# An FFT filter and two MLPs: the inverse transform in program order, with GpSimd issuing only DMAs there

## The chip, the cores and the metric

The kernel runs on 1 core of one Trainium2 chip. The metric is the device time of one execution in microseconds; lower is better. The kernel before took 1181.16 us (median of 3 runs, 1179.31 to 1184.85).

## The reference

```python
X = np.fft.rfft(x, axis=1)                        # x: 2 x 3008 x 256
Yr = Xr @ w_r - Xi @ w_i + b_r
Yi = Xr @ w_i + Xi @ w_r + b_i
Y = softthreshold(Yr, 0.01) + 1j * softthreshold(Yi, 0.01)
y = np.fft.irfft(Y, n=3008, axis=1)               # 6016 tokens x 256
h = y @ w_in;  y = (h * sigmoid(1.702 * h)) @ w_out    # 256 -> 2048 -> 256
h = y @ w_in2; y = (h * sigmoid(h)) @ w_out2           # 256 -> 2048 -> 256
```

All of it is float32, and the weights and the filter come as inputs.

## The kernel before

Everything is one program on one core, in four stages. The **forward** stage and the **mid** stage (the 512-wide complex product, threshold, folds) come first; then comes the **inverse** stage, which this case is about, and then the **MLP** stage, which is most of the time.

The inverse runs 16 steps, counted here 0 to 15: two column halves q, two batches b, four products t. `inv_mm` (line 598 on) makes one step's product into two PSUM banks. Steps with t = 0 and 1 use one pool of four banks, those with t = 2 and 3 the other, so a step can only begin where the step four earlier (same t, one batch before) has had its banks read. A step of q = 0 is 16 float32 matmul records of 188 to 192 columns, one of q = 1 is 12 of 376. Its result is taken off by `inv_post`, one step later in the program: for t = 0 and 1 of q = 0 by a ScalarE copy to `eo` (line 639; there is one `eo` buffer) and two VectorE combinations into `rt` (lines 647 and 384); for t = 0 and 1 of q = 1 by two ScalarE copies to `rt` (line 634); for t = 2 and 3 by four VectorE operations on `ac` and `rt` (lines 658, 659). There is one `rt` buffer. When four steps of a batch are done, `inv_out` writes `yt`, the tokens of that batch half: two of its four parts as sums or differences (line 689, on VectorE or GpSimd by the table `ivf`), two as a ScalarE copy (line 691) onto which a GpSimd-issued accumulating DMA adds the other operand (line 693).

In the same stretch two other jobs go on. One converts MLP weights, unit by unit: a 512 KB load into `raw` on the SP queue (line 166; one buffer), a ScalarE operation (line 175), five VectorE operations (lines 180 to 184), an accumulating DMA (line 237), and then the split into a rounded `hi` and a remainder `lo`. For units of `wo` the remainder is a ScalarE negation and an accumulating DMA (lines 105 to 107); for units of `wi` it is a GpSimd subtraction (lines 109, 110) ahead of which stand four small VectorE sums (lines 212 to 215, into `tmp`). The other prepares the first token block of the MLP: `xsums` and `xprep` (lines 706 on) make seven inputs k = 0 to 6, each split in `hi` and `lo`; k = 2, 3 and 5 share the buffer `tmp`, which is updated between them (line 727). `xprep` with k = 0 to 3 is called in the steps that the table `xi` names (11, 12, 13, 15), with `lo` made by ScalarE and an accumulating DMA (lines 722, 723); k = 4, 6 and 5 are called inside the first MLP group, with `lo` made by a VectorE subtraction (line 725).

What sets the order: the mid stage is in program order on all engines. In the inverse only TensorE is; the instructions of the other engines are placed by a scheduler, which reaches across the borders of the steps and of the stages. So is the first group of the MLP. From the second group on all is in program order.

The inverse-stage matrices `m` of q = 1 (four loads of 564 KB on the SP queue, line 137) are called for in steps 1 and 3.

Of the kernel before, what the change touches and what calls it, by code (L numbers as in the profile page):

```python
# [8 lines left out]

F32 = mybir.dt.float32  # L10
CFG = {'lv0': 'V', 'lv': 'VVVVVPVVVVVP', 'dd0': 'VPVVPPPPPVVP', 'dd': 'VVVVVVVVVVPV', 'ths': 'VVVVPV', 'thf': 'VVVP', 'ivf': 'VVVPVVVV', 'cva': 'P', 'pol': 'PPPP', 'pil': 'P', 'mvl': 'PVVP', 'xl': 'V', 'xse': 'V', 'gl': 'VPPPPPPP', 'tf': [6, 9, 12], 'tm': [2, 6, 10], 'ti': [1, 4, 7, 10], 'kb': [0, 1, 1, 1, 1, 1, 1, 0], 'kr': [0, 1, 0, 1, 0, 1, 1, 0], 'fa': 3, 'xp': [2, 4, 4, 5], 'xq': [1, 4, 1], 'xs': 4, 'xi': [11, 12, 13, 15], 'xsi': 9, 'ca': 4, 'tl': True, 'fwd': 'Pool,SP', 'rest0': 'all', 'rest1': 'all', 'last1': 'all', 'inv': 'PE', 'mid': 'all', 'last0': 'all', 'thm': 'A', 'gl0': 'PVPVVVPV', 'gl2': 'PPPPPPPP', 'gl3': 'PPPPPPPV', 'xl0': 'V', 'xl1': 'V', 'pre': 14, 'pre2': 0, 'yd': 6, 'lvb': 6, 'mlp': 'none', 'pr': 'VVVP', 'pf': 'PV', 'eo': '0010', 'n32': 2, 'li': [8, 10], 'xa': 4, 'nhb': 6, 'ddb': 6, 'mlp1': 'all', 'mlp2': 'all'}
NUM = dict(li=[5, 6, 7, 8], n32=2, pk=4, ydp=2, lii=[1, 3], xd=4, nhb=6, tf=[5, 9, 13], tm=[1, 3, 5, 7, 9, 11], ti=[0, 2, 4, 6, 8, 10, 12, 14, 14, 15, 15], kb=[2] * 8, kr=1, fa=3, fe=2, pm=0, nf=4, lvb=6, ddb=8, ivb=1, eob=1, fsb=6, f1=3, f2=0, fm=[7, 8, 9], fi=[1, 1, 2, 2], pre=13, pre2=1, yd=3, psh=0, ie=[12], xp=[1, 3, 4, 5], xq=[1, 2, 2], xs=5, nw=4, xi=[14, 14, 15, 15], xsi=13, rw=2, ca=4, cc=2, tb=1, tmn=1)

DEF = dict(pr="V", pf="V", lv0="V", lv="VPP", dd0="VVVVVP", dd="VPV", mpl="PV", ths="VP", thf="VVPP", fsl="VP", ivf="PPVV", cva="P", pol="P", pil="P", mvl="V", xl="PPVVPPP", xl0="PPVVPPP", xl1="PPVVPPP", xse="VP", gl="P", gl0="P", gl2="P", gl3="P", wcl="V", thc="V", thm="V")
F32R = mybir.dt.float32r
# [1 line left out]
AF = mybir.ActivationFunctionType  # L17
# [4 lines left out]
P = 128  # L22
# [34 lines left out]
def spectral_mlp_kernel(ctx, tc, xin, mfwd, minv, wc, bias, w_in1, w_out1, w_in2, w_out2, outT):  # L57
    nc = tc.nc
# [187 lines left out]
    def window(k, done, now=False):  # L246
        for u, a in done:
            if u[0] == "in":
                sums, puts = place_in(u[1], u[2], a, E('pil', u[2]), sums_tmp)
                if now:  # L250
                    for f in (puts[0], *sums, puts[1]):
                        f()
                else:
                    fill.extend(sums + puts)
            else:
                place_out(u[1], u[2], a, "D")
        for _ in range(min(k, len(loaded))):
# [453 lines left out]
    def xprep(l, i, k, part=3):  # L711

        n = blocks[i][1]
        (b11, t3), (b21, b22) = xhalves(i)
        src = (b11, b21, xtmp[0], xtmp[0], t3, xtmp[0], b22)[k]
        if part & 1:
            xb[l, i, k] = tuple(slot(0, F32R, "x")[:, :n] for _ in range(2))
            nc.scalar.copy(xb[l, i, k][0], src)  # L718
        if part & 2:
            hi, lo = xb[l, i, k]  # L720
            if (l, i) == (0, 0) and k < N('xd'):
                nc.scalar.mul(lo, src, -1.0)
                nc.gpsimd.dma_start(out=lo, in_=src, accum_op=ALU.add)
            else:
                E('xl1' if l else 'xl0' if i == 0 else 'xl', k).tensor_sub(lo, src, r32(hi))  # L725
            if k in (2, 3):
                nc.vector.tensor_sub(xtmp[0], b22 if k == 2 else b21, xtmp[0])

    prev = None
    for q in range(2):  # L730
        for b in range(B):
            for t in range(4):
                ps = inv_mm(q, b, t)
                if prev is not None:
                    inv_post(*prev)
                    if ydone:
                        inv_out()
                prev = (q, b, t, ps)
                if 8 * q + 4 * b + t == N('pre'):
                    tc.keep_in_program_order(nc.scalar.preload_act_table(AF.Gelu_apprx_sigmoid))  # L740
                step = 8 * q + 4 * b + t
                if step in N('lii'):
                    load_m()
                if step == N('xsi'):
                    xsums(0, 0)
                for k in range(4):
                    if N('xi')[k] == step:
                        xprep(0, 0, k)
                if step in N('ti'):
                    tick(N('ti').count(step))  # L750
    inv_post(*prev)
    inv_out()

    region('mlp')


    acc = {}
# [134 lines left out]
    for at, (l, i, p) in enumerate(seq):  # L892
        if (l, i, p) in ((0, 0, 1), (0, 0, 2)):
            region(f'mlp{p}')
        if (i, p) == (1, 0):
            region(f'rest{l}')
        if (i, p) == (last, 0):
            region(f'last{l}')
        nxt = (l, i + 1) if i < last else (1, 0)
        more = p == NPR - 1 and (l, i) != (1, last)  # L900
        k = rate(at)

        def hook(h):
            if more:
                if h in (1, 2):
                    for x in ((0,), (1, 2))[h - 1]:
                        xprep(*nxt, x)
                if h == 3:
                    xprep(*nxt, 3, 1)
                if h == 4:  # L910
                    xprep(*nxt, 3, 2)
            if p == 0:
                for x in {1: (4,), 3: (6, 5)}.get(h, ()):
                    xprep(l, i, x)
            if h == 1 and p == NPR - 2 and (l, i) != (1, last):
# [166 lines left out]
```

## Time and profile before

| | |
|---|---|
| median of 3 runs | 1181.16 us (1179.31 to 1184.85) |
| the profiled execution | 1180.89 us, of which the span of the trace is 1179.0 us |
| busy: TensorE / ScalarE / VectorE / GpSimd | 98% / 66% / 54% / 43% of the span |
| forward and mid stage | 0 to 138.5 us |
| inverse stage on TensorE | 138.5 to 195.4 us |
| MLP stage | 195.4 us to the end |

The span is cut by the work of TensorE (PE in the rows; PEld is its weight load). In the MLP stage it waits for almost nothing; its idle time stands in the forward stage and in the two places where the inverse hands over to itself (at 165 us) and to the MLP (198 to 204 us). VectorE is DVE in the rows, ScalarE is ACT, GpSimd is POOL.

### The profile page before, as it was taken

To read this page: it belongs to the slowest core of one execution; us is meant where nothing else is said; L and a number is where in the kernel's file an instruction comes from. 1 tells how busy PE (TensorE), PEld (TensorE's weight loads), DVE (VectorE), ACT (ScalarE), POOL (GpSimd) and SP (SyncE) were. 2 spreads that over 40 slices of the span, in tenths; PEclk is the share of its full clock that TensorE was granted. 3 is DMA by queue.
4 is the path that set the end of the run, shared out by engine and by line. 5 is a ranking of instruction groups with operands and counts; after the bars stand their busy time and mean duration, and the time that the engine had idled before them with its cause. 6 is when DMAs were issued, how large, how long until landed. Compare 5 with 4: busy or idle time off the path is not lost.

```text
span 1179.0 us, 14496 instructions
## 1 busy us (share of the span) xinstructions
PE 1153.6 (98%) x5036; PEld 941.2 (80%) x5036; DVE 633.2 (54%) x968; ACT 773.2 (66%) x1455; POOL 507.8 (43%) x433
## 2 busy tenths in 40 slices
PE   7999988999999999999999999999999999999998
PEld 3758865887888878878889978888888888888897
DVE  6838897776556366465564552442532622523522
ACT  2467445777667667667677776676665766766755
POOL 2336364444444444434446755433333433433333
PEclk9999999999999999999999999999999999999999
DMA  7556468332221221121120100010000000000000
GB/s 268 180 99 144 148 117 159 75 86 45 57 57 32 70 63 46 36 72 36 41 76 24 58 10 27 1 37 1 1 37 1 16 21 1 36 1 1 36 1 32
DMA packets 37259, 66.30 MB, mean 56 GB/s; under 512 B 3393, under 2 KB 14657, under 8 KB 37186
## 3 DMA queue, kind: packets, MB, share of 16 engines
q1 hardware_dynamic: 25730, 46.28, 11.7%
q0 software_dynamic: 11456, 19.10, 9.6%
q8 instruction: 39, 0.64, 0.2%
q14 instruction: 34, 0.28, 0.1%
HBM read 35.92 MB, written 10.35 MB: 39 GB/s over the span
## 4 chain that ended last, share of the span: by engine, by line
PE 85%; DVE 5%; DMA 4%; ACT 3%; issue 2%; POOL 1%; SPq 0%; DVEq 0%; POOLq 0%; ACTq 0%
PE o L772 39%; PE x L800 35%; PE psm L515 5%; PE psf L354 4%; ACT yt L803 1%; PE psm L512 1%; DMA raw<-in_x 1%; DMA raw<-in_wo 1%; PE psi L354 1%; ACT g L805 1%; DMA raw<-in_wi 1%; DMA x<-tmp 1%; DVE lv L302 1%; DVE cv_c L180 0%; DVE g L810 0%
## 5 line engine op out<-in xcount | busy, mean ns | idle before, releaser
L810 POOL TENSOR_TENSOR g<-yt,g 128x512 fp32r<-128x512 f32 (+1 forms) x282 | 363.5, 1301 | 503.9 <-PE x L800 315.1
L772 PE MATMUL o<-g,wo 128*128 128x512 f32 (+1 forms) x2304 | 560.9, 385 | 0.6 <-DMA wo<-cv_a 0.6
L800 PE MATMUL x<-x,wi 128*128 128x512 f32 (+1 forms) x2016 | 500.9, 387 | 8.3 <-ACT yt L836 3.7
L772 PEld LDWEIGHTS o<-g,wo 128*128 128x128 f32 x2304 | 432.7, 188 | 82.4 <-DMA wo<-cv_a 1.0
L800 PEld LDWEIGHTS x<-x,wi 128*128 128x128 f32 x2016 | 377.4, 188 | 86.9 <-ACT yt L836 7.8
L803 ACT ACTIVATE yt<-yt 128x512 f32<-128x512 f32 (+1 forms) x288 | 179.0, 622 | 251.0 <-DVE yt L842 198.8
L805 ACT CAST g<-yt 128x512 fp32r<-128x512 f32 (+1 forms) x384 | 234.9, 612 | 12.1
L842 DVE TENSOR_TENSOR yt<-yt,x 128x512 f32<-128x512 f32 (+1 forms) x96 | 64.7, 674 | 215.2 <-PE x L800 214.5
L821 DVE TENSOR_TENSOR yt<-yt,x 128x512 f32<-128x512 f32 (+1 forms) x96 | 64.8, 675 | 165.6 <-ACT yt L819 160.0
L810 DVE TENSOR_TENSOR g<-yt,g 128x512 fp32r<-128x512 f32 (+1 forms) x102 | 71.4, 700 | 71.3 <-ACT g L805 70.5
L354 PE MATMUL psf<-m,xf 128*128 128x376 f32 (+2 forms) x208 | 58.9, 444 | 8.4 <-DVE xf L313 8.2
L845 DVE TENSOR_TENSOR yt<-yt,x 128x512 f32<-128x512 f32 (+1 forms) x96 | 64.8, 675 | 3.3 <-PE x L800 2.7
L725 DVE TENSOR_TENSOR x<-yt,x 128x512 fp32r<-128x512 f32 (+1 forms) x46 | 47.9, 1044 | 29.1 <-ACT x L718 29.1
L354 PEld LDWEIGHTS psf<-m,xf 128*128 128x128 f32 x208 | 38.1, 194 | 28.5 <-DVE xf L313 9.4
L803 ACT ACTIVATE yt<-x 128x512 f32<-128x512 f32 (+1 forms) x96 | 56.0, 583 | 0.2 <-PE x L800 0.2
L354 PE MATMUL psi<-m,f 128*128 128x376 f32 (+3 forms) x208 | 52.1, 406 | 3.9 <-DVE rt L384 3.9
L836 ACT COPY yt<-x 128x512 f32<-128x512 f32 (+1 forms) x96 | 55.8, 581 | 0.0
L819 ACT COPY yt<-x 128x512 f32<-128x512 f32 (+1 forms) x96 | 54.8, 570 | 0.9 <-POOL g L810 0.9
L834 ACT COPY yt<-x 128x512 f32<-128x512 f32 (+1 forms) x96 | 54.8, 571 | 0.0
L354 PEld LDWEIGHTS psi<-m,f 128*128 128x128 f32 x208 | 37.2, 194 | 17.4 <-DVE rt L384 4.8
L237 POOL DMA_DIRECT2D cv_a<-cv_c x32 | 30.4, 952 | 33.4 <-DVE cv_c L184 14.9
L394 ACT COPY xt<-psf 128x128 f32<-128x128 f32 (+2 forms) x96 | 18.2, 286 | 33.2 <-PE psf L354 33.0
(105 smaller groups left out, 838.9 us busy)
## 6 DMA issues: line engine op xcount, KB each, us to landing
raw<-in_wi SPq DMA_DIRECT2D x32, 256.0 KB, 3.2
cv_a<-cv_c POOLq DMA_DIRECT2D x32, 256.0 KB, 3.4
raw<-in_wo SPq DMA_DIRECT2D x16, 512.0 KB, 3.8
raw<-in_x SPq DMA_DIRECT2D x12, 512.0 KB, 5.0
xl<-xt POOLq DMA_DIRECT2D x20, 256.0 KB, 4.3
out_t<-yt SPq DMA_DIRECT2D x20, 256.0 KB, 2.0
m<-in_mf SPq DMA_DIRECT2D x4, 564.0 KB, 5.6
m<-in_mi SPq DMA_DIRECT2D x4, 564.0 KB, 8.6
```

The source lines that it names most:

```text
L354: nc.tensor.matmul(ps, hi[:, c : c + P], m[:, k, :w], start=i == 0, stop=i == last)
L515: nc.tensor.matmul(t, st, mv, start=n == 0 and k == 0, stop=n == 3 and grp == 1 and k == 2)
L772: nc.tensor.matmul(acc[h, mm], st, mv, start=first and k == 0, stop=last and k == 2)
L800: nc.tensor.matmul(ps, st, mv, start=first and m == 0, stop=m == 2, skip_group_check=True)
L803: nc.scalar.activation(g, g if src is None else src, func)
L805: nc.scalar.copy(gh, g)
L810: eng.tensor_sub(gl, g, r32(gh))
L819: nc.scalar.copy(y1, X)
L821: nc.vector.tensor_add(y1, y1, Y)
L836: nc.scalar.copy(y3, X)
L842: nc.vector.tensor_add(y2, y2, X)
L845: nc.vector.tensor_add(y3, y3, Z)
```

## The change

1. The inverse stage is in program order on every engine (`inv` from 'PE' to 'all'). The first MLP group stays with the scheduler.
2. GpSimd gets no arithmetic there. The split of `wi` units uses the way of the `wo` units ("D": two ScalarE operations and an accumulating DMA), and all sums of `inv_out` are VectorE's (`ivf` = 'V').
3. All seven `xprep` of the first block are called inside the inverse, in steps 9, 10, 8, 11, 12, 14, 13 for k = 0 to 6 (`xsums` in step 8), all with a DMA for `lo`; the update of `tmp` stands ahead of k = 3 and 5.
4. The weight units are spread otherwise: up to six queued VectorE operations are issued in each step (`pi`), and a load of `raw` is called for two steps behind the conversion, not with it.

```diff
-CFG = {... 'ivf': 'VVVPVVVV', ... 'xi': [11, 12, 13, 15], 'xsi': 9, ... 'inv': 'PE', ...}
+CFG = {... 'ivf': 'V', ... 'xi': [9, 10, 8, 11, 12, 14, 13], 'xsi': 8, ... 'inv': 'all', ...}
...
-                sums, puts = place_in(u[1], u[2], a, E('pil', u[2]), sums_tmp)
+                sums, puts = place_in(u[1], u[2], a, "D" if modes[0] else E('pil', u[2]), sums_tmp)
...
+        if (l, i) == (0, 0) and k in (3, 5):
+            nc.vector.tensor_sub(xtmp[0], b22 if k == 3 else b21, xtmp[0])
...
-            if (l, i) == (0, 0) and k < N('xd'):
+            if (l, i) == (0, 0):
                 nc.scalar.mul(lo, src, -1.0)
                 nc.gpsimd.dma_start(out=lo, in_=src, accum_op=ALU.add)
+                return
...
-                for k in range(4):
-                    if N('xi')[k] == step:
+                for k, at in enumerate(N('xi')):
+                    if at == step:
                         xprep(0, 0, k)
+                pump(N('pi'))
                 if step in N('ti'):
-                    tick(N('ti').count(step))
+                    ready = settle()
+                    window(0, ready)
+                    window(1, ())
+                if step - 2 in N('ti'):
+                    cv_load(1 - len(loaded))
...
-            if p == 0:
+            if p == 0 and (l, i) != (0, 0):
                 for x in {1: (4,), 3: (6, 5)}.get(h, ()):
                     xprep(l, i, x)
```

Three places show how the instructions move. Names are those of the program: `psi` is a product in PSUM, `raw_...` a weight unit, and lines behind the change are one to ten higher than before (648 was 647, 692 was 691, 721 was 718).

VectorE where the mid stage ends and the inverse begins, before:

```order
L647 TENSOR_TENSOR rt<-psi,eo 128x2x2x95
L548 TENSOR_TENSOR f_1288<-th 128x512
L180 TENSOR_SCALAR cv_c<-cv_c 128x512
L384 TENSOR_TENSOR rt<-psi,eo 128x4x94
L181 TENSOR_SCALAR cv_c<-cv_c 128x512
L658 TENSOR_TENSOR ac<-rt,psi 128x377 x2
```

and after:

```order
L548 TENSOR_TENSOR f_1288<-th 128x512
L180 TENSOR_SCALAR cv_c<-cv_c 128x512
L181 TENSOR_SCALAR cv_c<-cv_c 128x512
L182 SCALAR_TENSOR_TENSOR cv_a<-raw_1170,cv_c 128x512
L183 TENSOR_SCALAR cv_c<-cv_a 128x512
L184 SCALAR_TENSOR_TENSOR cv_c<-raw_1170,cv_c 128x512
L648 TENSOR_TENSOR rt<-psi,eo 128x2x2x95
L384 TENSOR_TENSOR rt<-psi,eo 128x4x94
```

The two combinations that free the first step's bank stood around the last fold and the first conversion; now all five conversions of `raw_1170` stand ahead of them.

ScalarE in the first steps of the inverse, before:

```order
L639 COPY eo<-psi 128x2x192 x3
L691 ACTIVATE yt<-ac 128x2x377
L691 COPY yt<-ac 128x2x376
L109 CAST wi_1349<-tmp 128x512
L175 ACTIVATE cv_c<-raw_1301 128x512
```

and after:

```order
L640 COPY eo<-psi 128x2x192
L175 ACTIVATE cv_c<-raw_1301 128x512
L640 COPY eo<-psi 128x2x192
L105 ACTIVATE wi_1346<-cv_a 128x384
L107 CAST wi_1346<-cv_a 128x384
L105 ACTIVATE wi_1346<-tmp 128x512
```

The operation that waits for the load of `raw_1301` now stands between the `eo` copies of steps 0 and 1. On the SP queue that load, which stood behind the four loads of `m`, now stands ahead of them.

GpSimd in the second half of the inverse after the change; between the subtractions for `wi_1219` and those of the MLP there are now 29 DMA issues in a row, where before there were 22 among six subtractions and sums:

```order
L106 DMA wo<-cv_a 128x512
L694 DMA yt<-ac 128x2x377
L694 DMA yt<-ac 128x2x188 x2
L726 DMA x<-tmp 128x512
L726 DMA x<-yt 128x512 x2
L237 DMA cv_a<-cv_c 128x512
L106 DMA wo<-cv_a 128x512
```

Here the three accumulates of a batch half, those of k = 2, 0 and 1 and two of the weights follow one another with nothing between.

## Rows read from the trace of the kernel before

**Rows 1.** The page, busy time, share and instructions by engine.

```profile
PE 1153.6 (98%) x5036; PEld 941.2 (80%) x5036; DVE 633.2 (54%) x968; ACT 773.2 (66%) x1455; POOL 507.8 (43%) x433
```

**Rows 2.** Busy time by stretch: stretch, length, each engine, clock, DMA share, GB/s.

```profile
core 0: us, PE busy (x) PEld busy (x) DVE busy (x) ACT busy (x) POOL busy (x), PEclk, DMA share, GB/s
153.00:166.00 13.00, 9.17 (x48) 7.93 (x49) 11.60 (x17) 4.25 (x8) 9.30 (x8) 1.00 0.64 120
166.00:170.00 4.00, 4.00 (x9) 2.15 (x8) 3.96 (x11) 2.16 (x5) 2.61 (x3) 0.57 0.74 184
...
196.00:204.00 8.00, 3.96 (x17) 2.64 (x16) 7.17 (x14) 4.08 (x7) 1.71 (x2) 1.00 0.59 134
204.00:208.00 4.00, 4.00 (x12) 3.11 (x11) 0.94 (x2) 2.96 (x6) 1.27 (x1) 0.57 0.00 0
```

**Rows 3.** Timeline of TensorE, start, length, shape, count, idle time before and releaser.

```profile
138.50 6.01 PE L354 MATMUL psi<-m,f 128*128 128x192 f32 x36
...
153.31 2.21 PE L354 MATMUL psi<-m,f 128*128 128x192 f32 x12 [0.43 <-DVE rt L384]
...
165.42 30.39 PE L354 MATMUL psi<-m,f 128*128 128x376 f32 x90 [3.52 <-DVE rt L384]
195.36 3.19 PE L800 MATMUL x<-x,wi 128*128 128x512 f32 x12
199.21 0.97 PE L800 MATMUL x<-x,wi 128*128 128x512 f32 x3 [0.66 <-ACT yt L819]
203.56 2.50 PE L800 MATMUL x<-x,wi 128*128 128x512 f32 x6 [3.39 <-DVE yt L821]
...
226.84 1.52 PE L800 MATMUL x<-x,wi 128*128 128x512 f32 x6
```

**Rows 4.** Timeline of VectorE, first steps of the inverse.

```profile
146.54 1.22 DVE L180 TENSOR_SCALAR cv_c<-cv_c 128x512 f32<-128x512 f32 x1
147.68 0.54 DVE L384 TENSOR_TENSOR rt<-psi,eo 128x376 f32<-128x376 f32 x1
148.14 1.04 DVE L181 TENSOR_SCALAR cv_c<-cv_c 128x512 uint32<-128x512 uint32 x1
149.10 0.99 DVE L658 TENSOR_TENSOR ac<-rt,psi 128x377 f32<-128x377 f32 x2
150.01 0.68 DVE L182 SCALAR_TENSOR_TENSOR cv_a<-raw,cv_c 128x512 uint32<-128x512 uint32 x1
...
152.39 0.41 DVE L183 TENSOR_SCALAR cv_c<-cv_a 128x512 uint32<-128x512 uint32 x1
```

**Rows 5.** Timeline of all engines, 160 us on: VectorE beside GpSimd.

```profile
158.34 2.19 DVE L180 TENSOR_SCALAR cv_c<-cv_c 128x512 f32<-128x512 f32 x1 [1.27 <-ACT cv_c L175]
158.81 3.07 POOL L693 DMA_DIRECT2D yt<-ac  x2
...
160.32 2.90 POOL L110 TENSOR_TENSOR wi<-tmp,wi 128x512 fp32r<-128x512 f32 x1
```

**Rows 6.** Timeline of ScalarE, an `eo` copy and an operation that waits for a load.

```profile
148.33 0.48 ACT L639 COPY eo<-psi 128x384 f32<-128x384 f32 x1 [6.15 <-DVE rt L384]
...
157.63 0.68 ACT L175 ACTIVATE cv_c<-raw 128x512 f32<-128x512 f32 x1 [0.51 <-DMA raw<-in_wo]
```

**Rows 7.** Chain that ended last, 130 us on: start, length, what.

```profile
154.13 3.48 DMA raw<-in_wo
...
187.19 6.35 DMA x<-tmp
```

**Rows 8.** DMA issues from 150 to 206 us: count, KB each, median us to landing.

```profile
q0 software_dynamic: 3936, 5.46, 60.8%
...
wo<-cv_a POOLq DMA_DIRECT2D x3, 256.0 KB, 3.3
...
x<-tmp POOLq DMA_DIRECT2D x2, 256.0 KB, 5.4
```

**Rows 9.** Busy time by stretch, two in which only accumulating DMAs run.

```profile
170.00:172.00 2.00, 2.00 (x8) 1.18 (x7) 2.00 (x7) 2.00 (x4) 0.42 (x1) 1.00 1.13 202
176.00:178.00 2.00, 2.00 (x8) 1.18 (x7) 1.82 (x5) 0.00 (x0) 2.00 (x3) 1.00 1.22 156
```

**Rows 10.** Timeline of the SP queue, the loads of `m`.

```profile
128.29 4.03 SPq L137 DMA_DIRECT2D m<-in_mi  x6
```

More of the change, by code (lines that the diff above doesn't have):

```diff
@@ L10 @@
 F32 = mybir.dt.float32
-CFG = {'lv0': 'V', 'lv': 'VVVVVPVVVVVP', 'dd0': 'VPVVPPPPPVVP', 'dd': 'VVVVVVVVVVPV', 'ths': 'VVVVPV', 'thf': 'VVVP', 'ivf': 'VVVPVVVV', 'cva': 'P', 'pol': 'PPPP', 'pil': 'P', 'mvl': 'PVVP', 'xl': 'V', 'xse': 'V', 'gl': 'VPPPPPPP', 'tf': [6, 9, 12], 'tm': [2, 6, 10], 'ti': [1, 4, 7, 10], 'kb': [0, 1, 1, 1, 1, 1, 1, 0], 'kr': [0, 1, 0, 1, 0, 1, 1, 0], 'fa': 3, 'xp': [2, 4, 4, 5], 'xq': [1, 4, 1], 'xs': 4, 'xi': [11, 12, 13, 15], 'xsi': 9, 'ca': 4, 'tl': True, 'fwd': 'Pool,SP', 'rest0': 'all', 'rest1': 'all', 'last1': 'all', 'inv': 'PE', 'mid': 'all', 'last0': 'all', 'thm': 'A', 'gl0': 'PVPVVVPV', 'gl2': 'PPPPPPPP', 'gl3': 'PPPPPPPV', 'xl0': 'V', 'xl1': 'V', 'pre': 14, 'pre2': 0, 'yd': 6, 'lvb': 6, 'mlp': 'none', 'pr': 'VVVP', 'pf': 'PV', 'eo': '0010', 'n32': 2, 'li': [8, 10], 'xa': 4, 'nhb': 6, 'ddb': 6, 'mlp1': 'all', 'mlp2': 'all'}
@@ L12 @@
-NUM = dict(li=[5, 6, 7, 8], n32=2, pk=4, ydp=2, lii=[1, 3], xd=4, nhb=6, tf=[5, 9, 13], tm=[1, 3, 5, 7, 9, 11], ti=[0, 2, 4, 6, 8, 10, 12, 14, 14, 15, 15], kb=[2] * 8, kr=1, fa=3, fe=2, pm=0, nf=4, lvb=6, ddb=8, ivb=1, eob=1, fsb=6, f1=3, f2=0, fm=[7, 8, 9], fi=[1, 1, 2, 2], pre=13, pre2=1, yd=3, psh=0, ie=[12], xp=[1, 3, 4, 5], xq=[1, 2, 2], xs=5, nw=4, xi=[14, 14, 15, 15], xsi=13, rw=2, ca=4, cc=2, tb=1, tmn=1)
+CFG = {'lv0': 'V', 'lv': 'VVVVVPVVVVVP', 'dd0': 'VPVVPPPPPVVP', 'dd': 'VVVVVVVVVVPV', 'ths': 'VVVVPV', 'thf': 'VVVP', 'ivf': 'V', 'cva': 'P', 'pol': 'PPPP', 'pil': 'P', 'mvl': 'PVVP', 'xl': 'V', 'xse': 'V', 'gl': 'VPPPPPPP', 'tf': [6, 9, 12], 'tm': [2, 6, 10], 'ti': [1, 4, 7, 10], 'kb': [0, 1, 1, 1, 1, 1, 1, 0], 'kr': [0, 1, 0, 1, 0, 1, 1, 0], 'fa': 3, 'xp': [2, 4, 4, 5], 'xq': [1, 4, 1], 'xs': 4, 'xi': [9, 10, 8, 11, 12, 14, 13], 'xsi': 8, 'ca': 4, 'tl': True, 'fwd': 'Pool,SP', 'rest0': 'all', 'rest1': 'all', 'last1': 'all', 'inv': 'all', 'mid': 'all', 'last0': 'all', 'thm': 'A', 'gl0': 'PVPVVVPV', 'gl2': 'PPPPPPPP', 'gl3': 'PPPPPPPV', 'xl0': 'V', 'xl1': 'V', 'pre': 14, 'pre2': 0, 'yd': 6, 'lvb': 6, 'mlp': 'none', 'pr': 'VVVP', 'pf': 'PV', 'eo': '0010', 'n32': 2, 'li': [8, 10], 'xa': 4, 'nhb': 6, 'ddb': 6, 'mlp1': 'all', 'mlp2': 'all'}
@@ L14 @@
+NUM = dict(li=[5, 6, 7, 8], n32=2, pi=6, pk=4, ydp=2, lii=[1, 3], xd=4, nhb=6, tf=[5, 9, 13], tm=[1, 3, 5, 7, 9, 11], ti=[0, 2, 4, 6, 8, 10, 12, 14, 14, 15, 15], kb=[2] * 8, kr=1, fa=3, fe=2, pm=0, nf=4, lvb=6, ddb=8, ivb=1, eob=1, fsb=6, f1=3, f2=0, fm=[7, 8, 9], fi=[1, 1, 2, 2], pre=13, pre2=1, yd=3, psh=0, ie=[12], xp=[1, 3, 4, 5], xq=[1, 2, 2], xs=5, nw=4, xi=[14, 14, 15, 15], xsi=13, rw=2, ca=4, cc=2, tb=1, tmn=1)
 DEF = dict(pr="V", pf="V", lv0="V", lv="VPP", dd0="VVVVVP", dd="VPV", mpl="PV", ths="VP", thf="VVPP", fsl="VP", ivf="PPVV", cva="P", pol="P", pil="P", mvl="V", xl="PPVVPPP", xl0="PPVVPPP", xl1="PPVVPPP", xse="VP", gl="P", gl0="P", gl2="P", gl3="P", wcl="V", thc="V", thm="V")
@@ L592, in spectral_mlp_kernel @@
     region('inv')
+    modes[0] = True
     yt_p = opened("yt", "right")
@@ L739, in spectral_mlp_kernel @@
                 if 8 * q + 4 * b + t == N('pre'):
-                    tc.keep_in_program_order(nc.scalar.preload_act_table(AF.Gelu_apprx_sigmoid))
+                    nc.scalar.preload_act_table(AF.Gelu_apprx_sigmoid)
                 step = 8 * q + 4 * b + t
@@ L754, in spectral_mlp_kernel @@
     region('mlp')
+    modes[0] = None
     acc = {}
```

## The prediction

> **What bounds the kernel now.** I read the page's busy line first: TensorE is busy for 1153.6 of 1179.0 us [rows 1], so a change to other engines can only give or cost TensorE's idle time, and the time it spends at the lower clock. The diff touches the inverse stage and the first MLP group, so I then read TensorE's timeline there [rows 3]. The inverse starts at 138.50, the MLP at 195.36, and the last row, 226.84, is a point at which the MLP runs without gaps; it is my reference point, 108 matmuls behind 195.36. In between TensorE waits 0.43 and 3.52 us for VectorE's combination, then 0.66 and 3.39 us at the start of the MLP: 8.0 us. The stretches [rows 2] add something that the waits do not show: from 166 to 170 and from 204 to 208 the granted clock is 0.57 in the mean, so for most of it the 1.2 GHz level and not the 2.4, while TensorE was busy throughout. Each stretch stands right behind one of the two waits of over 3 us and costs 4 x 0.43 = 1.7 us, together 3.4. The wait of 0.43 us was followed by nothing of the kind.
>
> What a step costs: 36 records in 6.01 us are 0.163 each, so 2.6 us for a step of q = 0. The 90 records from 165.42 to 195.36 took 29.9 us, less 1.7 for the clock, so 0.314 each and 3.77 us for a step of q = 1. An MLP matmul is 0.227 (six in 1.52, of which some 0.16 is the tail of the last). With no wait the reference point would be at 138.5 + 8 x 2.6 + 8 x 3.77 + 108 x 0.227 = 214.0. It is at 226.8, so the most that this change can win is 12.8 us, and 11.4 of these are named above.
>
> **Part by part: what is removed.** GpSimd's sums and subtractions go. Beside them VectorE's conversions are stretched: L180, which takes 1.22 beside a subtraction at 146.54, takes 2.19 at 158.34 beside GpSimd's row L693 and L110 [rows 4, 5], where L183 of the same shape and kind takes 0.41. That stretch stands ahead of the combination for which TensorE waits 3.52 us, so this wait has its cause removed. The chain to the MLP's start has a DMA of `tmp` that is on it for 6.35 us [rows 7]; behind it stand the last takings-off of the inverse and the 3.39 us. With all seven inputs ready earlier, that goes too. The VectorE subtractions for k = 4, 5, 6 go; TensorE's own work stays.
>
> **What is added.** Of DMAs: four accumulates for the two `wi` units (2 x 448 KB) and three of 256 KB, 1.66 MB, on a queue that moved 5.46 MB between 150 and 206 us and took 60.8% of the engines' time for it [rows 8]. At the same cost per byte that is another 18 points. The four loads of `m` were issued at 128.29 to 132 [rows 10], in a quiet stretch; now they stand behind the load of `raw_1301` and fall on 151 to 163. On VectorE `inv_out` gains three sums, on ScalarE the new splits cost two operations each instead of one; both have room on average, and what they cost is order. So I walked the new order row by row: an instruction starts when its engine is free and what it waits for has ended, with the durations of the rows.
>
> Station 1, steps 4 and 5. VectorE begins the conversions at 146.1 (146.54 less one combination at a pitch of 0.46, which no longer stands ahead). Five of them take 1.22 + 1.04 + 0.68 + 0.41 + 0.68 [rows 4], so with the hand-overs they end at 150.2; only then come the two combinations of 0.54, to 151.3. The second half of step 4 needs that bank and could have begun at 138.5 + 4.5 x 2.6 = 150.2: **1.1 us**. The load of `raw_1301` is issued at 150.2 too, since its buffer is read until then. It took 3.48 us when nothing stood beside it [rows 7]; with an accumulate and the loads of `m` beside it I take 4.3. ScalarE's L175, 0.68 long, waits for it and stands ahead of the `eo` copy of step 1, 0.48 [rows 6], so step 5 begins at 155.6 and not at 152.6: **3.0 us**. In the order of before that operation stood behind three `eo` copies, so the same landing cost nothing.
>
> Station 2, the clock. A wait of 3.0 us is near the two that were followed by the lower clock and far from the 0.43 that was not; I count it once, **1.7 us**, with zero as the other end. Steps 5 and 6 then end at 162.5.
>
> Station 3, steps 7 and 8. VectorE from 155.7: two combinations, four sums of a quarter width, four operations of line 658's kind (a pitch of 0.5), five conversions (now at 0.41 and 0.68), then two more of the first kind, on which step 7 waits: 163.8, **1.3 us**. ScalarE then waits for the load of the next unit, issued at 162.7, and the `eo` copy behind it ends at 167.3 instead of 166.4: **0.9 us**.
>
> Station 4, step 10. The combinations of step 5 stand behind four ScalarE operations for `wi_1423` and end at 172.2. The conversions behind them wait for a `cv_a` buffer that an accumulate, new in this place, still reads until about 174.4; step 10 begins at 177.5, not 175: **2.5 us**.
>
> Station 5, step 15. From 182 on GpSimd issues 377 + 2 x 188 + 5 x 256 KB of accumulates in a row, 2.0 MB. The rates of such stretches are 202 and 156 GB/s [rows 9], so they take 10 to 13 us, and the last, which holds a `cv_a` buffer, lands at 195 to 198. I take 197. The conversions of `raw_1546` wait for it, and behind them on VectorE stand the operations that free step 15's bank: it begins at 200.1, not 196.4: **3.7 us**, and the clock again, **1.8**. The MLP begins at 205.9 instead of 195.4.
>
> Station 6, the first group. Its inputs are there except k = 5, which is used last. I find 2.4 us of waits up to the reference point, for ScalarE's copies behind the last split and for the accumulate of k = 6, where before there were 7.0 (226.84 - 195.36 - 24.5). The reference point is at 205.9 + 24.5 + 2.4 = 232.8.
>
> **Sum.** 232.8 against 226.8 is +6.0 us. Walked in the same way, the order of before gets to the reference point 1.0 us early, so the walk's own difference is +7.0; I take **+6.5**. Behind this point the orders are the same. The profiled span goes from 1179.0 to 1185.5. The execution is 1.9 longer than its span and the median 0.3 longer than that execution, so 1187.7.
>
> Of a single accumulate, two rows show medians of 3.3 and 5.4 us to landing [rows 8], and I used the upper side where several queue. The Trainium skill, "DMA: Bandwidth & Descriptors", section "Anatomy of one DMA", gives a fixed 2.0 us plus the bytes at 436 GB/s, by which 256 KB land in 2.6. The trace disagrees: no median here is as short. By that rule Stations 4 and 5 all but vanish and the time would be about 1179, an estimate from that page.
>
> **Rivals.**
>
> Accumulates land early. If they queue less than I think and land in the 3.3 us of the shorter row, no conversion waits for a `cv_a` buffer: Stations 4 and 5 lose 2.5 + 3.7 + 1.8 = 8.0 us, and the time is 1179.7; with half of it, 1183.7. For it: the `wo` accumulates of the same stretch landed in 3.3 us [rows 8]. Against it: the queue gets 1.66 MB more. Not slower, then; it decides at the point where the eight accumulates of Station 5 end before 193.4, the time at which VectorE asks for the buffer. Chance 0.20.
>
> Order harmless, relief whole. The load of `raw_1301` lands in 3.5 us, the wait at step 5 comes to 2.2 and the clock stays up, and the accumulates land early as well: a further 0.8 + 1.7 + about 4 of smaller waits on the same landings, so 1173 (1171 to 1175). For it: VectorE's stretched operations are the largest single loss before. Against it: Station 1 rests on two facts of the order, not on a size. Chance 0.21.
>
> The queue is worse. At 156 GB/s for all accumulates, or if a GpSimd issue takes the 1.5 us of the two L693 in 3.07 us [rows 5], the walk comes out 4 to 6 us later: 1192 to 1194. The Trainium skill, "SBUF — State Buffer", section "SBUF: two separate sides", says that VectorE in a mode that takes both ports keeps GpSimd from writing its descriptors, which speaks for this case; the row with 3.07 stands beside such an operation, but also among GpSimd's own arithmetic. Chance 0.13.
>
> The change doesn't do what it says. The listings show that it does; what could remain is that it cancels: 1181. Chance 0.04.
>
> **How the numbers follow.** Forecast 1187.7, own range 1183.5 to 1191, chance 0.42. The range that should hold 8 times in 10 leaves out the lower half of the order-harmless case and the upper end of the worse queue: 1173 to 1194. About 0.5% is what a measurement of this kernel can tell from no change, so slower begins at 1187.1 and faster ends at 1175.3. Slower: 0.28 of the forecast's 0.42 and all of the worse queue, 0.41. Same: the rest of the forecast, 0.14, the early landing, 0.20, and the cancelling, 0.04, 0.38. Faster: 0.21.
>
> **What would show it.** In the profile after, TensorE's waits in the inverse should be several, of 1 to 4 us: one on ScalarE's `eo` copy near 152 to 156, with L175 in front of that copy waiting for `raw<-in_wo`; one on VectorE near 175 to 178; one near 197 to 200 with a conversion waiting for a DMA that wrote `wo`. VectorE's conversions should take 0.4 to 0.7 throughout after 150. The MLP should start at 200 to 206 and lose under 3 us. I am wrong on Station 1 if step 5 starts before 154, on Stations 4 and 5 if steps 9 to 15 follow without gaps, and on the sign if the MLP starts before 199.

## The result, and the profile after

| | before | after |
|---|---|---|
| median | 1181.45 us (6 runs, 1179.31 to 1184.85) | 1194.07 us (6 runs, 1192.86 to 1195.34) |
| after / before | | 1.0106, 95% interval 1.0090 to 1.0122 |
| span of the profiled execution | 1179.0 us | 1191.8 us |
| inverse begins on TensorE | 138.50 | 138.80 |
| MLP begins | 195.36 | 211.67 |
| reference point, 108 matmuls later | 226.84 | 239.43 |

The change made the kernel 12.6 us slower, the way the forecast said, but by twice as much: 1187.7 was forecast, and 1194.07 lies just outside the range that ended at 1194. Nearly all of it is lost before the reference point: 12.6 us there, 12.8 over the span.

The page's busy line of the changed kernel answers to [rows 1]. TensorE's busy time grew by 3.8 us with the same number of matmuls, 1.2 of them ahead of the inverse, so part of the loss is matmuls that took longer, the rest is waiting:

```profile
PE 1157.4 (97%) x5036; PEld 943.7 (79%) x5036; DVE 629.3 (53%) x968; ACT 776.0 (65%) x1462; POOL 505.2 (42%) x433
```

TensorE's timeline after (start, length, shape, count, in brackets the idle time before and what released it) answers to [rows 3]:

```profile
138.80 6.01 PE L354 MATMUL psi<-m,f 128*128 128x192 f32 x36
...
152.15 1.57 PE L354 MATMUL psi<-m,f 128*128 128x192 f32 x8 [1.55 <-DVE rt L384]
156.11 2.87 PE L354 MATMUL psi<-m,f 128*128 128x192 f32 x16 [2.40 <-ACT eo L640]
159.34 0.89 PE L354 MATMUL psi<-m,f 128*128 128x190 f32 x4 [0.36 <-DVE rt L660]
...
167.07 0.97 PE L354 MATMUL psi<-m,fd 128*128 128x190 f32 x2 [4.92 <-DVE rt L660]
...
181.56 19.19 PE L354 MATMUL psi<-m,f 128*128 128x376 f32 x60 [1.31 <-issue]
205.86 6.25 PE L354 MATMUL psi<-m,f 128*128 128x376 f32 x12 [5.11 <-DVE rt L660]
211.67 4.10 PE L810 MATMUL x<-x,wi 128*128 128x512 f32 x16
217.20 2.11 PE L810 MATMUL x<-x,wi 128*128 128x512 f32 x8 [1.43 <-DMA x<-yt]
...
239.43 2.20 PE L810 MATMUL x<-x,wi 128*128 128x512 f32 x9
```

With one more of 0.55 at 220.09 the waits are 17.6 us; before they were 8.0. Two of them, 4.92 ahead of step 7 and 5.11 ahead of step 15, are more than all the others together. Where they come from stands in VectorE's timeline, L182 being the conversion that writes `cv_a`:

```profile
159.69 0.55 DVE L660 TENSOR_TENSOR rt<-rt,psi 128x377 f32<-128x377 f32 x1
160.15 0.42 DVE L180 TENSOR_SCALAR cv_c<-cv_c 128x512 f32<-128x512 f32 x1
160.60 0.43 DVE L181 TENSOR_SCALAR cv_c<-cv_c 128x512 uint32<-128x512 uint32 x1
164.00 0.69 DVE L182 SCALAR_TENSOR_TENSOR cv_a<-raw,cv_c 128x512 uint32<-128x512 uint32 x1 [2.97 <-DMA wi<-cv_a]
...
166.37 0.55 DVE L660 TENSOR_TENSOR rt<-rt,psi 128x377 f32<-128x377 f32 x1
...
178.54 0.69 DVE L182 SCALAR_TENSOR_TENSOR cv_a<-raw,cv_c 128x512 uint32<-128x512 uint32 x1 [2.21 <-DMA wi<-cv_a]
...
199.18 0.43 DVE L181 TENSOR_SCALAR cv_c<-cv_c 128x512 uint32<-128x512 uint32 x1
202.89 0.69 DVE L182 SCALAR_TENSOR_TENSOR cv_a<-raw,cv_c 128x512 uint32<-128x512 uint32 x1 [3.28 <-DMA wo<-cv_a]
```

Each time L182 stands still until a DMA has landed that does not write for it, but reads the buffer that it is to overwrite: an accumulate has `cv_a` as its source, and there are two such buffers. (The row at 178.54 is the same ahead of step 10.) Behind L182, in program order, stand the operations L659 and L660 that free the bank TensorE wants. The accumulates are late because the DMA engines are full at those moments. These are the issues of the changed kernel from 156 to 157.5 us and, the second row, from 190 to 196 (columns: tile, queue, count, size of each, median us from issue to landing):

```profile
wi<-cv_a POOLq DMA_DIRECT2D x1, 192.0 KB, 7.0
```

```profile
wo<-cv_a POOLq DMA_DIRECT2D x1, 256.0 KB, 9.6
```

The stretches (columns as in [rows 2]) show the clock:

```profile
153.00:166.00 13.00, 6.38 (x37) 5.53 (x35) 6.70 (x16) 2.99 (x6) 1.72 (x2) 1.00 0.90 262
166.00:170.00 4.00, 2.93 (x9) 2.96 (x10) 3.75 (x7) 1.85 (x3) 1.41 (x2) 0.50 0.42 135
170.00:182.00 12.00, 10.69 (x34) 7.10 (x34) 7.19 (x17) 4.20 (x9) 6.24 (x7) 0.88 0.86 133
182.00:196.00 14.00, 14.00 (x46) 8.46 (x45) 10.74 (x20) 7.86 (x15) 8.62 (x9) 1.00 0.96 175
...
204.00:208.00 4.00, 2.14 (x4) 1.27 (x5) 3.86 (x8) 2.22 (x5) 2.61 (x4) 0.50 0.73 158
208.00:212.00 4.00, 4.00 (x11) 2.25 (x10) 3.90 (x8) 3.89 (x9) 3.47 (x4) 0.71 1.12 215
```

The 1.2 GHz level again stands behind the two long waits, but lasts longer than in [rows 2]: half of 2.93, 0.12 x 12, half of 2.14 and 0.29 x 4 are 5.1 us, where before it was 3.4. The whole way from the inverse's begin to the reference point, first before and then after, in the same columns:

```profile
138.50:226.84 88.34, 80.27 (x334) 60.70 (x332) 73.33 (x119) 46.42 (x85) 46.29 (x42) 0.96 0.57 114
138.80:239.43 100.63, 82.89 (x333) 62.44 (x332) 68.91 (x119) 49.30 (x92) 43.39 (x42) 0.93 0.65 135
```

TensorE is idle for 8.1 us before and 17.7 after. So of the 12.6 us, 9.7 are waits, 2.6 are matmuls that took longer, of which the clock in the stretches above accounts for 1.7, and 0.3 is the later begin.

### The profile page after: what moved, and what is told of

The parts are those of the page before. It is cut to its first block, busy times and chain, and to the rows that moved or that the text cites. A ratio compares the mean times of both kernels' runs of the same rounds, so it can differ in the third digit from the quotient of the medians.

```text
span 1191.8 us, 14513 instructions
## 1 busy us (share of the span) xinstructions
PE 1157.4 (97%) x5036; PEld 943.7 (79%) x5036; DVE 629.3 (53%) x968; ACT 776.0 (65%) x1462; POOL 505.2 (42%) x433
## 3 DMA queue, kind: packets, MB, share of 16 engines
q0 software_dynamic: 12464, 20.80, 10.3%
## 4 chain that ended last, share of the span: by engine, by line
PE 81%; DMA 5%; issue 4%; DVE 4%; ACT 3%; POOL 1%; SPq 0%; POOLq 0%; DVEq 0%; ACTq 0%
PE o L782 39%; PE x L810 34%; PE psf L354 5%; PE psm L515 2%; ACT yt L813 1%; PE psm L512 1%; DMA wo<-cv_a 1%; DMA raw<-in_wi 1%; DMA wi<-cv_a 1%; ACT g L815 1%; DMA x<-yt 1%; DMA raw<-in_wo 1%; POOL yt L694 1%; DMA raw<-in_x 1%; DVE f L548 1%
## 5 line engine op out<-in xcount | busy, mean ns | idle before, releaser
L354 PE MATMUL psi<-m,f 128*128 128x376 f32 (+3 forms) x208 | 55.5, 423 | 10.7 <-DVE rt L660 5.5
L354 PEld LDWEIGHTS psi<-m,f 128*128 128x128 f32 x208 | 39.6, 205 | 25.4 <-DVE rt L660 5.7
L175 ACT ACTIVATE cv_c<-raw 128x512 f32<-128x512 f32 x32 | 21.5, 672 | 40.4 <-DMA raw<-in_wo 28.2
L237 POOL DMA_DIRECT2D cv_a<-cv_c x32 | 31.5, 983 | 34.1 <-DVE cv_c L184 18.9
```

The costliest lines, as they stand in the source:

```text
L354: nc.tensor.matmul(ps, hi[:, c : c + P], m[:, k, :w], start=i == 0, stop=i == last)
```

## The experiments

The theory after reading this: in a fixed order a late landing costs whatever stands behind the instruction that waits for it, and the two landings that cost most are accumulates that hold a `cv_a` buffer. The rivals: the volume of the queue sets the pace wherever things stand, or the fixed order costs without any DMA.

All medians are beside runs of the kernel before on the same chip; the ratio is to those. The kernel before took 1181.45 us beside the changed kernel, 1183.03 beside the first three experiments and "units one step later", and 1182.2 to 1182.4 beside the others, so a difference of medians between kernels that were not run together is good to some 1.5 us. In a kernel with an edit in the helpers the line numbers are a few higher. The last two columns are read from each kernel's TensorE timeline: the length of the inverse, and from the MLP's begin to the reference point (24.5 us without a wait).

| kernel | us | to before, 95% interval | inverse | to the reference point |
|---|---|---|---|---|
| before | 1181.45 | | 56.9 | 31.5 |
| after | 1194.07 | 1.0106 (1.0090 to 1.0122) | 72.9 | 27.8 |
| two more buffers | 1188.87 | 1.0056 (1.0041 to 1.0071) | 62.6 | 32.6 |
| `m` loads early | 1191.00 | 1.0076 (1.0060 to 1.0092) | 69.0 | 27.7 |
| no accumulates for x | 1188.56 | 1.0051 (1.0035 to 1.0068) | 68.8 | 27.6 |
| units one step later | 1195.00 | 1.0110 (1.0094 to 1.0125) | 65.7 | 35.3 |
| change with scheduler | 1187.12 | 1.0035 (1.0023 to 1.0047) | 51.5 | 42.0 |
| order alone | 1201.41 | 1.0152 (1.0137 to 1.0167) | 70.3 | 37.7 |
| wi on GpSimd | 1189.34 | 1.0064 (1.0045 to 1.0082) | 68.8 | 27.2 |
| three together | 1183.13 | 1.0005 (0.9996 to 1.0014) | 64.3 | 27.0 |
| five together | 1179.57 | 0.9967 (0.9953 to 0.9981) | 59.9 | 26.6 |
| second unit later still | 1185.88 | 1.0030 (1.0020 to 1.0041) | 60.4 | 32.7 |
| the same, wi on GpSimd | 1186.00 | 1.0036 (1.0024 to 1.0048) | 60.4 | 32.6 |
| L175 with conversions | 1173.83 | 0.9934 (0.9920 to 0.9947) | 53.7 | 27.2 |

### Two more buffers

```diff
-        a = cv_p.tile([P, 2 * CU], F32, tag="a", name="cv_a")
+        mine = modes[0] and taken[0] < 2
+        taken[0] += bool(mine)
+        a = slot(0, F32, "cv_a") if mine else cv_p.tile([P, 2 * CU], F32, tag="a", name="cv_a")
```

> The changed kernel (1194.07 us), with the converted weights (cv_a) of the first two units of the inverse written to two free buffers of the x inputs, so that no conversion there has to wait until an accumulate has read its buffer; every instruction and every DMA stays. Theory A (the two largest waits, 4.92 us before step 7 and 5.11 us before step 15, come from VectorE's L182 waiting 2.97 and 3.28 us for such a buffer, with the operations that free the step's bank behind it): L182 follows L181 without a gap, the wait before step 7 falls to about 2 us and that before step 15 to under 2 us, at least one of the two stretches at the lower clock goes, and the time is 1185 to 1188. Theory B (the queue of accumulates itself is what is late, and the next to need one of them, ScalarE's L105 or L175, waits instead): the waits only move, 1191 to 1194.

It came out at 1188.87, 5.2 us below the changed kernel. VectorE's timeline has no gap left ahead of the conversion (L185 here), and TensorE's two waits are 1.99 and 2.30:

```profile
160.25 0.43 DVE L184 TENSOR_SCALAR cv_c<-cv_c 128x512 uint32<-128x512 uint32 x1
160.72 0.69 DVE L185 SCALAR_TENSOR_TENSOR cv_a<-raw,cv_c 128x512 uint32<-128x512 uint32 x1
```

```profile
163.78 0.56 PE L357 MATMUL psi<-m,fd 128*128 128x190 f32 x2 [1.99 <-DVE rt L663]
...
197.30 4.06 PE L357 MATMUL psi<-m,f 128*128 128x376 f32 x12 [2.30 <-DVE rt L663]
```

So theory A holds for the cause of both waits: no DMA was taken away, only the need to wait for it. Its sizes were a little too good, 2.30 against "under 2" ahead of step 15 and 0.9 us more than its range in all. The inverse is 10.3 us shorter. Half of that is given back right behind it: the first group now waits 2.81 us for an accumulate of x and 1.66 for ScalarE, since the landings did not come forward as far as the matmuls did. That part is theory B's.

### The m loads early

```diff
     mid_fold(*thr)
     pump()
+    load_m()
+    load_m()
     cv_load(1 - len(loaded))
```

> The changed kernel with the four loads of m (2.26 MB) called for ahead of the load of raw_1301, so that they are issued at about 129 us, as in the kernel before, and not at 151.5. Theory A (these loads share the DMA engines with the first accumulate that reads cv_a, which took 7.0 us to land and holds the buffer for L182): it lands in 3.5 to 4 us, the wait of 4.92 us before step 7 falls to about 2, the wait of 2.40 before step 5 to about 2, and the time is 1188 to 1191. Theory B (the landing is long because GpSimd writes its descriptors late, not for lack of room on the DMA engines): it stays over 6 us and the time at 1193 to 1195.

1191.00, at the upper edge of theory A. The accumulate that took 7.0 us to land takes 2.9, and the wait ahead of step 7 is 2.04 instead of 4.92:

```profile
wi<-cv_a POOLq DMA_DIRECT2D x1, 192.0 KB, 2.9
```

```profile
164.38 0.56 PE L354 MATMUL psi<-m,fd 128*128 128x190 f32 x2 [2.04 <-DVE rt L662]
...
178.91 20.88 PE L354 MATMUL psi<-m,f 128*128 128x376 f32 x60 [3.31 <-issue]
```

So it was the four loads of `m`, which the change put behind `raw_1301` on the SP queue, that made this landing late, not GpSimd's writing of it. The second row shows why only 3.1 us came back: the wait ahead of step 10 grew from 1.31 to 3.31, on the next buffer.

The Trainium skill, "DMA: Bandwidth & Descriptors", section "Anatomy of one DMA", gives a fixed 2.0 us plus the bytes at 436 GB/s, for this accumulate of 192 KB an estimate of 2.45 us. With the DMA engines busy 0.30 of the time from 156 to 160 us the 2.9 of this run comes near; beside the `m` loads the 7.0 does not.

### No accumulates for x

```diff
             if (l, i) == (0, 0):
-                nc.scalar.mul(lo, src, -1.0)
-                nc.gpsimd.dma_start(out=lo, in_=src, accum_op=ALU.add)
+                nc.vector.tensor_sub(lo, src, r32(hi))
                 return
```

> The changed kernel with the seven lo parts of x made by a VectorE subtraction of 128x512 (0.69 us each) instead of a ScalarE operation and an accumulating DMA of 256 KB: 1.8 MB less on GpSimd's queue from 187 us on, 4.8 us more on VectorE, 4.4 us less on ScalarE. Theory A (the volume on the queue makes the accumulate wo<-cv_a land after 9.6 us, and that holds step 15): it lands in 4 to 6 us, the wait before step 15 falls from 5.11 to under 2 us, the stretch at the lower clock behind it and the wait of 1.43 in the MLP go, and the time is 1186 to 1189. Theory B (the fixed order is what costs, whatever the queue carries): VectorE's work stands ahead of the same operations, 1192 to 1196.

1188.56, as theory A said. The accumulate `wo<-cv_a` that took 9.6 us lands in 5.7, L182 does not wait for it, and step 15 begins after a wait of 1.85; the wait ahead of step 7, with which x has nothing to do, is as long as ever:

```profile
wo<-cv_a POOLq DMA_DIRECT2D x1, 256.0 KB, 5.7
```

```profile
168.43 0.97 PE L354 MATMUL psi<-m,fd 128*128 128x190 f32 x2 [5.21 <-DVE rt L660]
...
204.01 4.06 PE L354 MATMUL psi<-m,f 128*128 128x376 f32 x12 [1.85 <-DVE rt L660]
```

The run also takes seven operations from ScalarE and puts 4.8 us of subtractions on VectorE; what these do by themselves it does not show.

### The remainders of wi on GpSimd

```diff
-                sums, puts = place_in(u[1], u[2], a, "D" if modes[0] else E('pil', u[2]), sums_tmp)
+                sums, puts = place_in(u[1], u[2], a, E('pil', u[2]), sums_tmp)
```

> The changed kernel (1194.07 us) with the remainders of the two wi units made by GpSimd's subtraction again, as in the kernel before, so four accumulates (0.9 MB) less on the queue and two subtractions a unit on GpSimd. Theory A (the accumulate that reads cv_a while the m loads go is what holds L182 before step 7): GpSimd reads cv_a directly and is done near 159, so that wait falls from 4.92 to about 2 us, the one before step 10 to under 1, and the time is 1188 to 1191; the waits near step 15 stay. Theory B (GpSimd's arithmetic stretches VectorE's conversions by as much as it saves, as before the change): 1193 to 1196.

1189.34, in theory A's range. Ahead of step 7 there is no wait at all: the only ones up to 168 us are 1.55 and 2.85, ahead of steps 4 and 5. The wait ahead of step 15 stays, at 4.67. So the accumulates that item 2 of the change brought in cost some 5 us. That it is because they hold a buffer, and not for their bytes, is shown by the two more buffers, with which L182 stopped waiting though every DMA stayed.

### Units one step later

```diff
-'ti': [1, 4, 7, 10]
+'ti': [2, 5, 8, 11]
```

> The changed kernel with the weight units taken up in steps 2, 5, 8 and 11 instead of 1, 4, 7 and 10. It moves L175 of raw_1301 behind the eo copies of steps 0 and 1, and the conversions behind the operations that free the banks of steps 3 and 13. No DMA is saved. Theory A (what costs is what stands in front of what; the waits on DMAs cost only since operations that free a bank stand behind them): the wait of 2.40 us before step 5 goes, the one before step 7 falls to under 2, the one before step 15 to under 2, and the time is 1184 to 1189. Theory B (the volume on the DMA engines and the landings set the pace of the stage, wherever the conversions stand): other steps wait instead, 1191 to 1196.

1195.00: theory B, this shift by itself gives nothing. The waits ahead of steps 5 and 7 are gone, as A said, but L182 meets the same unlanded accumulate one step on, and step 8 waits instead (rows below). The inverse is 7.1 us shorter all the same, but the first group takes 7.5 longer, with waits of 2.92 us for ScalarE and 2.94 for an accumulate of x:

```profile
165.79 0.69 DVE L182 SCALAR_TENSOR_TENSOR cv_a<-raw,cv_c 128x512 uint32<-128x512 uint32 x1 [3.03 <-DMA wi<-cv_a]
```

```profile
168.77 4.13 PE L354 MATMUL psi<-m,f 128*128 128x376 f32 x6 [4.65 <-DVE rt L384]
```

### The order alone, and the change without the order

The kernel before with `'inv': 'all'` (and the table load of ScalarE where program order has it), and the changed kernel with `'inv': 'PE'`.

> The kernel before with nothing changed but the inverse in program order on every engine. Its program issues the five conversions of a unit in the step in which ScalarE's L175 waits for the load, ahead of that step's successors, and the m loads stand behind raw_1301. Theory A (the order alone costs more than the change as a whole): TensorE waits behind L175 and the conversions in most of the four units, 2 to 5 us each, and the time is 1190 to 1205. Theory B (the order is harmless, the new DMAs cost): 1179 to 1185.

> The changed kernel with the inverse given back to the scheduler on every engine but TensorE, as in the kernel before; the accumulates for wi, the sums on VectorE and all seven inputs of x inside the inverse stay. Theory A (it is the program order that turns late landings into waits of TensorE): the scheduler places other work where the order waits, and the time is 1180 to 1186. Theory B (the 1.66 MB more on the queue cost as much in any order): 1190 to 1196.

The order alone takes 1201.41, theory A: the old program, written for a scheduler, has L175 and all five conversions in one step. It needs no new DMA to wait. Its L182 also waits for GpSimd's subtraction, which holds the same kind of buffer:

```profile
158.30 2.93 PE L354 MATMUL psi<-m,f 128*128 128x192 f32 x8 [3.31 <-ACT eo L639]
...
179.36 31.46 PE L354 MATMUL psi<-m,f 128*128 128x376 f32 x90 [5.09 <-DVE rt L384]
```

```profile
175.32 1.74 DVE L182 SCALAR_TENSOR_TENSOR cv_a<-raw,cv_c 128x512 uint32<-128x512 uint32 x1 [3.33 <-POOL wi L110]
```

The change with the scheduler takes 1187.12, between what the two theories said. Its inverse is the shortest of all, 51.5 us with one wait of 0.32, so in that order the new accumulates make TensorE wait for next to nothing there. What the scheduler put off it pays at the MLP's begin, where ScalarE's L175 waits 8.34 us for a load, with `yt` of the first group behind it:

```profile
202.00 0.66 ACT L175 ACTIVATE cv_c<-raw 128x512 f32<-128x512 f32 x1 [8.34 <-DMA raw<-in_wo]
```

```profile
205.26 1.65 PE L810 MATMUL x<-x,wi 128*128 128x512 f32 x3 [10.76 <-ACT yt L829]
```

### Three, five, and L175

The three edits of the first experiments in one kernel; then with them the units one step later and `pump` from step 1 on only, without the call of it that stood ahead of the inverse, so that the conversions of `raw_1170` stand behind the first two combinations (cut):

```diff
     mid_fold(*thr)
-    pump()
+    load_m()
+    load_m()
...
-                pump(N('pi'))
+                if step:
+                    pump(N('pi'))
```

> The changed kernel with the two more buffers, the m loads early and the seven lo parts of x on VectorE, together. Alone these gave 5.2, 3.1 and 5.5 us. If each of them took away a wait of its own the time is 1180.3. Since the first and the second take the same wait before step 7, and the first and the third the same before step 15, I expect 1184 to 1187: the waits of 1.55 before the second half of step 4 and of 2 to 2.5 before step 5 stay, one stretch at the lower clock, and little else.

> As the three together, with the units one step later (steps 2, 5, 8, 11) and the conversions of raw_1170 behind the first two combinations of the inverse instead of ahead of them. Theory A (the two waits that are left near 152 and 156 come from what stands in front: the conversions in front of the combinations, L175 in front of the eo copy): both go, nothing takes their place since the buffers are there, and the time is 1178 to 1182. Theory B (each unit's chain of load, conversion and accumulate is as long as the steps between two units, so that a later start only moves the waits): 1184 to 1188.

Three together give 1183.13, 0.9 below the expected stretch and level with the kernel before (the interval holds 1). Not expected in it was a wait of 3.02 us ahead of step 15, with buffers and without the accumulates of x: ScalarE's L175 waits 4.70 us for its load there, with a cast of x behind it that VectorE needs. Five give 1179.57, theory A: neither wait is there any more. "One step later", worth nothing alone, is worth 3.6 us together with the later conversions of `raw_1170` once the buffers are there; no run separates the two. One long wait is left, and it is again ScalarE's L175 (L178 here), waiting for its load with an `eo` copy behind it:

```profile
168.15 0.66 ACT L178 ACTIVATE cv_c<-raw 128x512 f32<-128x512 f32 x1 [8.02 <-DMA raw<-in_wo]
168.72 0.46 ACT L644 COPY eo<-psi 128x384 f32<-128x384 f32 x1
```

```profile
169.23 29.84 PE L357 MATMUL psi<-m,f 128*128 128x376 f32 x84 [4.21 <-ACT eo L644]
```

Two ways to get it out of the way. The first takes the units later still, `'ti': [2, 6, 9, 12]`, and a second kernel has GpSimd's subtraction for wi besides:

> As the five together (1179.57 us), with the units in steps 2, 6, 9 and 12 instead of 2, 5, 8 and 11. There one wait of 4.21 us is left, before step 9, with 1.7 us at the lower clock behind it: ScalarE's L175 of the second unit waits for its load and stands ahead of the eo copy of step 5. With step 6 it stands behind that copy. Theory A (again what stands in front): wait and clock go, 1172 to 1176. Theory B (the units end later, and the last reaches into the MLP's first group): what is won is given back there, 1177 to 1181.

> As the one before it, with the remainders of the wi units by GpSimd's subtraction instead of two ScalarE operations and an accumulate. Theory A (with the buffers there, no conversion waits for the accumulates of wi, so they cost nothing; GpSimd's subtractions stretch VectorE's operations beside them): 0 to 3 us slower than with the accumulates. Theory B (0.9 MB less on the queue brings the other landings forward): 1 to 4 us faster.

They take 1185.88 and 1186.00, over 6 us more than the five. The wait ahead of step 9 is gone, but the third unit's L175 now stands ahead of the copies that free the banks for q = 1, and TensorE waits 3.70 us for those; the last units reach into the MLP's first group, which takes 32.7 us and not 26.6. That is theory B in kind, but its range ended at 1181: I had both sizes wrong. Between the two kernels there is no difference that can be told: where no conversion waits for a buffer, the accumulates of wi cost no more than GpSimd's subtractions in their place.

The second way moves L175 alone, into the list from which the conversions are issued:

```diff
-        nc.scalar.activation(c, hf, AF.Abs, scale=2.0**-112)
+        first = lambda: nc.scalar.activation(c, hf, AF.Abs, scale=2.0**-112)
+        if modes[0]:
+            fill.append(first)
+        else:
+            first()
```

> As the five together (1179.57 us, units in steps 2, 5, 8 and 11), with ScalarE's L175 of a unit issued together with that unit's conversions, one or two steps later, so that in the second unit it stands behind the eo copies of steps 4 and 5. There one wait of 4.21 us is left, before step 9, with 1.7 us at the lower clock behind it. Theory A (the position of L175 alone makes that wait): both go and the conversions, which wait for L175 anyway, don't move on VectorE; 1173 to 1176. Theory B (the load of raw lands so late that with L175 the conversions of that unit now hold the operations of step 7 that free a bank, one step further): 1178 to 1181.

1173.83, theory A, and faster than both kernels: 0.9934 of the one before, 20 us below the changed one. TensorE's waits in the inverse are these two, the MLP begins at 192.99, and the granted clock stays at 1.00 from 138 to 228 us:

```profile
163.56 13.53 PE L361 MATMUL psi<-m,f 128*128 128x376 f32 x42 [1.59 <-DVE rt L391]
178.02 15.43 PE L361 MATMUL psi<-m,f 128*128 128x376 f32 x48 [0.93 <-ACT rt L643]
192.99 5.93 PE L818 MATMUL x<-x,wi 128*128 128x512 f32 x24
```

## Why the prediction was right in kind and wrong in size

**Station 1: right.** Step 4 lost 1.55 us (1.1 forecast), since the five conversions of `raw_1170` took 5.3 us, not 4.0. The first three, in VectorE's timeline of the changed kernel:

```profile
145.55 1.49 DVE L180 TENSOR_SCALAR cv_c<-cv_c 128x512 f32<-128x512 f32 x1
147.08 1.10 DVE L181 TENSOR_SCALAR cv_c<-cv_c 128x512 uint32<-128x512 uint32 x1
148.27 1.58 DVE L182 SCALAR_TENSOR_TENSOR cv_a<-raw,cv_c 128x512 uint32<-128x512 uint32 x1
```

They are stretched as in [rows 4, 5], for GpSimd still ran the last fold and the subtractions of `wi_1219` beside them. Step 5 lost 2.40 (3.0). The load of `raw_1301`, issued at 151.11, was there at 155.03, with L175 ahead of the `eo` copy exactly as the order showed. Five together, with both put behind, has neither wait.

**Station 2: wrong place, and too small.** No lower clock followed the wait of 2.40; it came after the next, and cost 2.9 us there instead of 1.7. That it stayed away behind step 5 was no rule of that wait: in the kernel without accumulates for x, whose edit acts from step 8 on, nearly the same wait at the same time was followed by the 1.2 GHz level. Its row in TensorE's timeline there, and the stretch behind it in the columns of [rows 2]:

```profile
156.11 5.19 PE L354 MATMUL psi<-m,f 128*128 128x192 f32 x20 [2.37 <-ACT eo L640]
```

```profile
158.00:160.00 2.00, 2.00 (x8) 2.00 (x7) 1.93 (x5) 1.14 (x2) 0.86 (x1) 0.50 1.03 366
```

**Station 3: the step that failed.** It priced VectorE's own work up to step 7 and got 1.3 us; measured were 4.92, with 2.9 of clock behind it. The walk had the `m` loads falling on 151 to 163 and had accumulates holding `cv_a` from Station 4 on, but did not put the two together: the first accumulate that reads `cv_a` is issued at 156.78, in the midst of those loads, and L182 asks for its buffer at 161.0. The term to add was the 2.97 us of that wait. Three runs show it: with other buffers, with the loads out of the way, and without the accumulate, the wait falls to 1.99, 2.04 and none.

**Step 8 and Station 4: right mechanism, too high.** Forecast 0.9 and 2.5; there was no wait ahead of step 8, and 1.31 ahead of step 10, where L182 did stand still for a `cv_a` buffer, for 2.21 us. That the wait of step 7 gave the later landings time fits the `m` loads early, where a shorter wait ahead of step 7 came with a longer one ahead of step 10.

**Station 5: right mechanism, too small.** 3.7 us forecast, 5.11 measured. The accumulate `wo<-cv_a` landed at 202.8 and not at 197: 9.6 us from its issue. The rates used, 156 to 202 GB/s, hold (175 from 182 to 196 us), but the row of accumulates began at 185.98 and not at 182, behind the delay of Station 3: 4.0 of the 5.8 us. The prediction's own 195 to 198 lies 3 us above 182 plus 10 to 13, and no row of it names them. Why TensorE's wait itself was 1.4 longer no run separates.

**Station 6: near.** 2.4 us of waits forecast, 2.0 measured.

**The sum.** The forecast had the MLP at 205.9; it began at 211.67. Of these 5.8 us, Station 3 and the clock behind it are 3.6 and 1.2, Station 5 and its clock 1.4 and 0.4; the rest, too high and too low, comes to -0.8.

**The rivals.** "Accumulates land early" and "order harmless" fell with the waits themselves. "The queue is worse" gave 1192 to 1194 and came nearest, but for half of its reason. With the `m` loads elsewhere the first accumulate landed in 2.9 us and not 7.0, so the DMA engines' load made it late; the second lies in a stretch in which they are busy 0.96 of the time. GpSimd's issues need not have been slow: these two of the changed kernel stand beside VectorE's L659 and L660, and beside L182, and took as little as any:

```profile
159.11 0.86 POOL L106 DMA_DIRECT2D wi<-tmp  x1 [1.48 <-ACT wi L105]
...
202.84 0.86 POOL L106 DMA_DIRECT2D wo<-cv_a  x1 [1.97 <-DMA wo<-cv_a]
```

The prediction cited for the other half the Trainium skill, "SBUF — State Buffer", section "SBUF: two separate sides", by which VectorE in a mode that takes both ports keeps GpSimd from writing descriptors. No row here shows it or rules it out: the issues that took over 2 us follow directly on another issue, and none that stands by itself runs wholly beside a conversion of L180's kind, which is what the prediction's row showed.

**What the change was for did happen.** From 150 us on the conversions take 0.42 to 0.69 us, and TensorE no longer waits for a stretched one. That relief is real, and the order and the DMAs that came with it cost more. L175 with conversions keeps the one and mends the other. Not run by themselves are the sums of `inv_out` on VectorE (item 2) and the other spread of the units (item 4).

## What to carry to other kernels

When a stage goes from a scheduler to program order, list for every instruction that can wait for a DMA what stands behind it on its engine, and count as such a wait not only data that must arrive but also a buffer that a DMA still reads: an accumulate holds its source until it lands. Price the landing by what else the queues carry at that moment, with the transfers that the change itself has moved there. Then mend it by position and buffers together: here one step's shift alone gave nothing, and more buffers alone gave back half of what they won.

## What was not expected of the hardware

An accumulate of 192 KB took 2.9 us to land on quiet DMA engines (busy 0.30) and 7.0 beside four loads of 564 KB; one of 256 KB took 9.6 in the run of accumulates from 186 us on.

The lower clock did not follow the length of a wait in any plain way: 2.40 us ahead of step 5 were followed by none in the changed kernel, 2.37 us at the same place without the accumulates for x by 0.50 from 158 to 160 us, and 1.99 us ahead of step 7 in the one with two more buffers were followed by a granted clock of 0.68 from 166 to 170 us. Whether the waits shortly before count too stays open; no run separates that.
